# A first transform stage that contracts 128 rows from 128-byte runs, with B's first half in two pieces and zero matmuls ahead of the data

## The chip, the cores and the metric

The kernel runs on one core of one Trainium2 chip. A core has TensorE (PE, matmuls into PSUM), VectorE (DVE), ScalarE (ACT), GpSimd (POOL), SyncE (SP, which here only issues transfers) and 16 DMA engines that all queues share. The metric is the time of one execution on the device in microseconds, the median over runs.

## The reference, cut to what matters

Two independent halves are computed on a sequence of 2048 steps with 640 channels and put side by side in the output, in bf16.

```python
# A: a diagonal state space with complex states
Lam_bar = exp(dt * Lam);  B_bar = ((Lam_bar - 1) / Lam)[:, None] * Bmat
h_t = Lam_bar * h_{t-1} + x_t @ B_bar.T
a = 2 * real(h @ Cmat.T) + x * Dskip
# B: a short shift convolution, a product, and a convolution as long as the sequence
kv = (sum_t k_pad[t : t + S] * shift_k[:, ks - 1 - t]) * v
y = irfft(rfft(kv, 2 S) * rfft(ssm_k, 2 S))[:S]
b = q * (y + kv * ssm_D)
out = concat([a, b], -1)
```

## The kernel before, in words

**Half A** works on 16 interleaved phases of the sequence. B is loaded with a transposing DMA (`a_B`, operations `B00` to `B11`: first digit the half of the 640 states, second digit real or imaginary part), x likewise (the first eight phases come plainly as `xn0`, `xn1` and are turned on TensorE by `px..`, emptied by `ex..`; the others as `x1..`, transposing DMAs). `a_unit` (line 646) projects: for ten groups j of states and two halves, `dn0_j_h` and `dn1_j_h` are ten matmuls each (line 658), `e1` empties PSUM, `m1` and `e3` combine phases by rotation matrices (`set_..`, line 416). A coarse scan (`S`, `jw`, `scan`, `jv`), a way down (`d1`, `d00` to `d02`, added by DVE in `a1`, `a0`) and the output projection `py` (line 801, emptied by `ey`, stored by `st`) follow. C is loaded by transposing DMAs `cn..` and scaled by `ct..`.

**Half B** goes in five groups G of 128 channels. The convolution over 2 x 2048 points is a transform in two stages, with tables made on the chip. For each group the filter (`h`) and the product (`k`) go through the same steps:
- `hst` (line 828) loads the filter from HBM, `dtap` (line 831) adds ssm_D to the first tap. `kvs`, `kvl` (lines 888, 890) write the product kv, which DVE and ACT made in `cv`, `cs`, `ca`, `cm`, to HBM and load it again, so that 64 partitions hold 8 channels times 8 stretches of time, twice.
- `s1` (line 894) is the first stage: four operations of 32 matmuls, each on 64 rows by 64 columns of the array (form 64*64), two accumulating on each result. `e1h`, `e1k` empty them on ACT or DVE through the helper `copy` (lines 237, 239).
- `s2` (line 919) is the second stage, 16 matmuls each of 128 rows by 64 columns (128*64), emptied by `e2`.
- `pP`, `pQ`, `pY` multiply the spectra, `i2` (64*128) and a transposing DMA `zt` and `i1` (128*64) go back, `ob` multiplies by q and stores.

**Order.** All operations go through a graph, but the order is a text, `ORDER` (line 146): a list of names. `x/A`, `x/D`, `x/G`, `x/S` name the engine where there is a choice, and the digits behind `@` are the buffers that the operation takes (PSUM pairs of banks, or one of seven SBUF buffers `s4` and six `s8`). `emit` issues each engine's share in the order of that list, so each engine, and each queue of transfers, works strictly in order. `halves` and `split` (lines 108, 120) let operations that can be run either way (`m1`, `d0`, `d1`, `S`, `jw`, `jv`; helper `mm`, line 227) take two matmuls of 128*64 instead of one of 128*128 where the operation before them on TensorE is of that form.

The tables of the first stage are made in `setup`: phases `w0`, `w1` (lines 449, 454), sines `w2` (470), masks `mk` (481), the table `R` (490), and `Ct` for the way back (498).

Of the kernel before, what the change touches and what calls it, by code (L numbers as in the profile page):

```python
# [9 lines left out]
ALU = mybir.AluOpType  # L10
ACT = mybir.ActivationFunctionType
# [30 lines left out]
class Graph:  # L42
# [77 lines left out]
    def halves(self, o):  # L120

        return True if o.name.startswith(("dn", "s2", "i1")) else False if o.name.startswith(("py", "px")) else None
# [24 lines left out]
ld_lre kz2/D@0 w0 xn0@0 scol pidx Dm0 B00 consts J0 w1 E0 kz1/G@1 ci0@1 w2 zero J1 c4 wi1@2 ld_lim ld_ldt xn1@2 wi0@3 bc  # L147
px00@0 B01 px02@1 wm1 nrow ex00/A ex02/A par@2 px04@3 p0 nrowf dtb Dm1/S wm0 B10 px10@0 ex04/A px12@1 E1 px14@2 p1 ex12/A nrho
x121 fi mk rn ph ci1 ld_sk/S dn0_2_0@4 x130 ex10/D trig dn0_0_0@6 B11 ex14/D ws1@4 R dn1_2_0 rc ss dn1_1_0@0 set_3_0/D
set_2_0/G dn1_0_0 e1_2_0/A dn1_4_0@2 set_1_0/D ws0@5 k0@6 kz0/G set_1_1/G x131 dn0_4_0 e1_0_0/D hst0/S@2 m1_2_0 x120 set_3_1/G  # L150
dn0_1_0 e3_2_0/D e1_4_0/D m1_0_0 dn1_8_0@4 ct@3 set_2_1/G e3_0_0/D e1_1_0/D dn0_8_0 sk x101 cv300/D@4 dn1_9_0@6 set_4_1/D
m1_1_0 dn0_9_0 cs200/D@3 v0@5 e1_8_0/A dtap0/D set_8_1/D m1_4_0 e3_1_0/A m1_8_0 e3_4_0/A ca200 s1h03@0,4 x100 e3_8_0/A s1h01@2
e1h03/A dn0_3_0@4 cs100/D x111 e1h01/A ca100 s1h00@0 x110 e1_9_0/A s1h02@2 cs000/D dn1_3_0 kz3/G@2 e1h00/A ca000 hst1/S@6
m1_9_0 e1h02/A dn1_7_0@0 cm00 e1_3_0/A s2h02@2,5 den kvs0/S dn0_7_0 e3_9_0/A k1 e2h02/A set_12_0/D s2h03@6 m1_3_0 g e2h03/A
dn0_4_1@2 e1_7_0/A s2h01@6 dn1_4_1 e2h01/A dtap1/D set_G_0/G set_8_0/D m1_7_0 e3_3_0/A kvl0/S@3 s1h10@6,0 e3_7_0/A k2 s1h12@4
e1h10/A set_G_1/D dn0_0_1@0 set_12_1/G e1h12/A s1h11@6 set_4_0/D dn1_0_1 e1_4_1/A ld_dsk/G e1h11/A m1_4_1 cv310/D@5 s1h13@4
e3_4_1/A cs210/D@4 v1@6 s1k03@6,2 e1h13/A dn0_1_1@2 ca210 e1k03/A s1k00@4 cs110/D e1_0_1/A s1k02@6 V dn1_1_1 e1k00/D e1k02/A
m1_0_1 ca110 e1_1_1/A s2h00@4 s1k01@6 e3_0_1/A cs010/D m1_1_1 e1k01/A dn1_3_1@0 cv320/D@3 e3_1_1/A ca010 s2k03@6,1 e2h00/A
dn0_3_1 cm10 e2k03/A s2k01@2,4 s2k00@4 e2k01/A kvs1/S dn1_2_1@6 e2k00/D k3 e1_3_1/A s2k02@2 pP00@6 s2h11@4,1 e2k02/A dn0_2_1
pQ00 e2h11/A m1_3_1 cn00@3 dn0_8_1@2 e3_3_1/A pP01@5 e1_2_1/A s2h12@4 s2h13@0 pY00 e2h12/A dn1_8_1 e2h13/A m1_2_1 pQ01  # L160
kvl1/S@4 i200@4,4 e3_2_1/A i201@0 e300/A pY01 S0@6 v2@6 e301/A dn1_9_1@4 cs220/D@1 eS0/A ca220 i202@0 e1_8_1/A i203@6 cn10
dn0_9_1 cs120/D e302/A ca120 e303/A s1k10@0,2 m1_8_1 cs020/D e1_9_1/A zt0@5 dn1_6_1@6 e3_8_1/D e1k10/A ca020 m1_9_1 s1k11@2
e3_9_1/A s1k13@0 cm20 e1k11/A s1k12@4 dn0_6_1 e1k13/A e1k12/D jw0@2 e1_6_1/A s2h10@0 q0/S@5 jsw0 dn0_7_1@4 cn11@0 e2h10/A Ct
jcw0 jaw00 scan0 hst2/S@0 s2k13@2,1 s2k12@0 e2k13/A dn1_7_1 e2k12/A dn1_5_0@2 e1_7_1/A s2k11@0,4 pP11@6 cn01 dn0_5_0 e2k11/A
pQ11 m1_7_1 s2k10@0 e3_7_1/A m1_6_1 e2k10/A pY11 dn1_6_0@4 e1_5_0/A i100@0 pP10@1 kvs2/S e3_6_1/A dn0_6_0 dtap2/G ob00 m1_5_0
s1h22@6,4 e3_5_0/A pQ10 e1_6_0/A s1h20@0 dn1_5_1@2 e1h22/A pY10 dn0_5_1 e1h20/A kz4/G@3 k4 diagD hst3/S@4 jv0@6 e1_5_1/A
i213@0,2 jsv0 m1_6_0 e313/A m1_5_1 i211@6 e3_5_1/D e3_6_0/A i212@0 jcv0 e311/A i210@2 kvl2/S@6 jav00 S5@4 v3@1 jav01 e312/A
e310/D d1_0@6 eS5/A ct00@0 a1_0 ct01@2 ect00/A jw5@4 jcw5 s1h23@6 ect01/A dtap3/D jsw5 ct10@0 e1h23/A ct11@2 jaw50 i101@4
scan5 ect11/A ct20@6 ect10/A s1h21@2 ect20/A s1k23@0,1 q1/S@0 ob01 e1h21/A d1_2@6 d1_3@7 a1_2 jv5@4 ob0/S e1k23/A ct21@2 zt1@5
jsv5 ect21/A ct30@0 jcv5 s1k21@4 jav51 ect30/A s1k22@2 jav50 d1_4@6 e1k21/A a1_3 d1_9@0 d1_5@1 a1_4 e1k22/A d1_7@7 a1_9 d1_6@6  # L170
ct31@4 a1_5 ct40@2 ect31/A d1_1@0 a1_6 d1_8@1 a1_7 ect40/A ct41@4 d00_6@6 a1_8 ect41/A d00_7@7 d00_0@2 a1_1 d00_5@3 cs230/A@5
d00_2@1 d00_8@0 a00_5 py0_32@4,0 a00_6 a00_2 py1_32 a00_7 a00_8 s1k20@6 ey_32/A a00_0 d00_9@3 d00_4@1 e1k20/A st_32/S d00_3@0
a00_9 d00_1@2 i111@4 a00_1 cv330/A@6 a00_3 i110@6 a00_4 s1h33@2,0 ca230 py0_03@0,1 e1h33/A ob11 cs130/A py1_03 ob10 py0_33@2,0
ey_03/A ca130 st_03/S ob1/S py1_33 cs030/D ca030 d01_1@4 s1h32@6 ey_33/A a01_1 s1h30@0 st_33/S e1h32/A cm30 d01_9@5 hst4/S@2
d01_3@4 py0_02@2,1 cv340/A@5 cs240/D@1 kvs3/S a01_9 py1_02 e1h30/A ca240 d01_0@5 py0_00@6,0 ey_02/D cs140/A a01_0 st_02/S
dtap4/G s2h20@0,3 a01_3 d01_8@5 s2k21@2,0 e2h20/A a01_8 d01_6@4 py1_00 kvl3/S@6 ca140 e2k21/A a01_6 s2k20@0 ey_00/A d01_5@5
d01_2@4 e2k20/A d02_6@2 st_00/G a01_5 s2h21@6 d01_4@3 a02_6 d01_7@5 e2h21/A py0_31@0,1 a01_7 cs040/A a01_2 s1k33@6,2 a01_4
s1k30@4 s1k32@2 pP20@3 e1k30/A py1_31 e1k32/A ca040 py0_12@4,0 e1k33/A pQ20 q4/S@1 ey_31/A py1_12 pY20 st_31/S d02_5@2 s2h23@6
v4@0 ey_12/A a02_5 d02_3@3 s2h22@0 e2h23/A a02_3 d02_1@2 d02_7@4 d02_2@5 a02_1 e2h22/A s1k31@6 st_12/S a02_2 d02_9@3 e1k31/A
s1h31@0 a02_9 d02_4@2 a02_7 d02_8@5 e1h31/A s2k22@6,6 d02_0@3 a02_8 e2k22/A i220@0,5 a02_4 i221@4 a02_0 e320/A s2h33@6,4 cm40  # L180
s2h30@2 py0_21@0,1 e2h30/A e2h33/D kvs4/S e321/A py1_21 s2k23@2 ey_21/A s2h32@6 e2k23/D st_21/S s1h40@4,1 e2h32/A s1h42@0
kvl4/S@4 pP21@3 s2k31@2,0 e1h42/A py0_20@6,0 e2k31/D e1h40/A s2k32@0,5 pQ21 s2k33@4 e2k32/A s2h31@2 py1_20 pY21 e2k33/A pP31@6
py0_22@0,1 ey_20/A e2h31/A st_20/S pQ31 s1h41@4 s1k40@6,0 pY31 s1h43@2 e1k40/A py1_22 q2/S@2 e1h41/D e1h43/A s2k30@6 ey_22/D
s2h41@2,3 e2k30/A i223@4 st_22/G e2h41/D s1k41@0 e323/A s1k42@6 pP30@5 py0_13@2,0 e1k42/A pQ30 e1k41/A py1_13 pY30 s1k43@4
i222@6 ey_13/D e1k43/A i231@0,2 e322/D st_13/S i232@2 e331/A s2k40@4,4 e332/D s2k41@6 zt2@4 e2k40/A s2h42@0 e2h42/D e2k41/A
s2h40@2 i230@4 e2h40/A i233@6 e330/D py0_30@0,1 e333/A pP40@0 s2h43@2 s2k42@4,3 pQ40 zt3@1 e2h43/A s2k43@6 py1_30 pY40 e2k42/A
e2k43/A py0_23@2,0 ey_30/A pP41@5 i121@4 pQ41 st_30/S q3/S@6 i240@6,0 i241@0 pY41 e340/A py1_23 e341/A i242@6 ey_23/A i243@0
e342/A st_23/G i120@2 e343/D py0_10@6,1 ob20 zt4@5 ob21 i131@0 i130@2 ob31 py1_10 ob30 ob2/S py0_11@4,0 ey_10/D st_10/S ob3/S
py1_11 i140@0 ey_11/A st_11/G i141@2 ob40 py0_01@6,1 ob41 py1_01 ob4/S ey_01/A st_01/S
# [3 lines left out]
class Kernel:  # L193
# [55 lines left out]
    def pre(self):  # L249
        op, v = self.op, self.nc.vector  # L250
        self.Dm = self.t([128, 80], bf16, "Dm")

        def f_Dm(e):
            v.memset(self.Dm[:], 0.0)
        op("Dm0", {"DVE": 0.1}, f_Dm, w=["Dm"])
        op("Dm1", {"SP": 0.4, "POOL": 1.2}, lambda e: self.eng[e].dma_start(
            out=self.Dm[0:128:16, :], in_=self.B_ssm_D.rearrange("(b c) -> c b", c=8)), w=["Dm"], dma=0.5)

    def setup(self):
# [69 lines left out]
        small("nrow", f_nrow, [], ["nrow"], 0.3, "POOL")  # L329
        small("nrowf", lambda: v.tensor_copy(out=nrowf[:], in_=nrow[:]), ["nrow"], ["nrowf"], 0.5)  # L330
# [112 lines left out]
        ws = T([128, 96], i32, "ws")  # L443
        rowa = T([128, 2], f32, "rowa")
        colw = T([128, 1], f32, "colw")
        pr = T([128, 2], i32, "pr")
        phs = T([128, 96], i32, "phs")

        def f_w0():
            g.iota(ws[:, 0:64], pattern=[[0, 2], [4, 32]], base=1, channel_multiplier=0)  # L450
            g.iota(ws[:, 64:96], pattern=[[1, 32]], base=0, channel_multiplier=0)
        small("w0", f_w0, [], ["ws"], 0.4, "POOL")

        def f_w1():
            v.tensor_single_scalar(out=pr[:, 0:1], in_=pidx[:], scalar=15, op=ALU.bitwise_and)
            v.tensor_single_scalar(out=pr[:, 1:2], in_=pidx[:], scalar=31, op=ALU.bitwise_and)
            v.tensor_scalar(out=rowa[:, 0:1], in0=pr[:, 0:1], scalar1=2.0, scalar2=0.0, op0=ALU.mult, op1=ALU.add)
            v.tensor_scalar(out=rowa[:, 1:2], in0=pr[:, 0:1], scalar1=2.0, scalar2=1.0, op0=ALU.mult, op1=ALU.add)
            v.tensor_scalar(out=colw[:], in0=pr[:, 1:2], scalar1=4.0, scalar2=1.0, op0=ALU.mult, op1=ALU.add)
            for a0 in range(2):  # L460
# [714 lines left out]
```

## Time and profile before

| what | value |
|---|---|
| median of 6 runs | 202.2 us (201.65 to 205.76) |
| the profiled execution | 201.83 us, its span 200.0 us |
| busy: PE, DVE, ACT, POOL | 186.9, 168.2, 148.1, 21.1 us |
| matmuls | 4042 recorded |
| s1 matmuls (L909) | 1280, 22.8 us |
| s2 matmuls (L945) | 640, 42.8 us in two groups |
| dn matmuls (L658) | 400, 49.8 us |
| packets on the queue of SP and ACT | 109668, 32.52 MB |

The span runs from the first to the last instruction; the 1.83 us outside it belong to the execution but to no instruction. A busy time of TensorE counts overlapping matmuls once, and their ends are modelled, so starts of one group and of the next are what tells its length. "Chain" is the list of work that ended last, followed back from the end: start, length, engine, tile and line. In the timeline, the last bracket of a line is the idle time of the engine before it and what ended it.

### The profile page before, as it was taken

The numbers are of one execution on the slowest core, as the hardware profiler recorded it, in microseconds if no ns is written. First come the engines' busy times: TensorE is split into PE (matmuls) and PEld (weight loads), VectorE is DVE, ScalarE is ACT, GpSimd is POOL, SyncE is SP. The second block draws the span as 40 slices with busy tenths as digits, with TensorE's granted clock in tenths as the row PEclk, the third lists the DMA queues.
The fourth block names the chain that finished last, engine by engine and source line by source line (L and its number), as shares of the span: only waits on it lengthen the run. The fifth ranks groups of instructions, "written<-read, shape, count | busy, mean of one in ns | idle before, by whom it ended". The sixth has DMA issues, their size and how long they took to land.

```text
span 200.0 us, 8858 instructions
## 1 busy us (share of the span) xinstructions
PE 186.9 (93%) x4042; PEld 138.2 (69%) x4043; DVE 168.2 (84%) x264; ACT 148.1 (74%) x175; POOL 21.1 (11%) x35
## 2 busy tenths in 40 slices
PE   0889999998999999799999999999999999999992
PEld 0756676656777677567657777677787878788771
DVE  7899899876889999959988999788959999977640
ACT  4999978996888888489976749896967678753011
POOL 8056500800000000000000000100000010001010
PEclk9999999999999999999999999999999999999999
DMA  6999996999989999969994058508334243998995
GB/s 172 264 156 191 190 167 155 240 147 139 215 209 208 167 237 200 261 136 215 226 207 107 5 147 252 136 26 184 94 143 108 76 101 90 185 221 186 202 239 143
DMA packets 109959, 33.74 MB, mean 169 GB/s; under 512 B 107106, under 2 KB 108642, under 8 KB 109922
## 3 DMA queue, kind: packets, MB, share of 16 engines
q1 hardware_dynamic: 109668, 32.52, 81.3%
q8 instruction: 31, 0.51, 1.0%
q0 software_dynamic: 224, 0.66, 1.0%
q14 instruction: 6, 0.05, 0.1%
q10 hardware_dynamic: 30, 0.00, 0.0%
HBM read 9.19 MB, written 7.86 MB: 85 GB/s over the span
## 4 chain that ended last, share of the span: by engine, by line
PE 69%; DMA 12%; ACT 7%; DVE 7%; issue 2%; SPq 1%; POOL 0%; POOLq 0%; DVEq 0%; ACTq 0%
PE ps L806 18%; PE ps L658 16%; PE ps L909 9%; PE ps L945 8%; DMA s<-kvd 5%; PE ps L1001 5%; PE ps L231 4%; DMA s<-s 4%; PE ps L233 4%; PE ps L1037 3%; DMA s<-in_B_ssm_k_dram 3%; ACT s L237 2%; PE ps L810 2%; DVE s L239 2%; DVE s L968 1%
## 5 line engine op out<-in xcount | busy, mean ns | idle before, releaser
L237 ACT CAST s<-ps 128x1024 bf16<-128x1024 f32 x86 | 84.0, 1018 | 16.6 <-PE ps L909 6.4
L658 PE MATMUL ps<-xT,BC 128*64 128x512 bf16 x400 | 49.8, 386 | 0.5 <-DVE xT L239 0.5
L806 PE MATMUL ps<-BC,hb 128*128 128x320 bf16 x240 | 36.4, 300 | 0.0
L658 PEld LDWEIGHTS <-BC 128*64 128x64 bf16 x400 | 24.0, 111 | 14.5 <-issue 1.9
L806 PEld LDWEIGHTS <-hb 128*128 128x128 bf16 x240 | 21.9, 98 | 8.7 <-issue 0.3
L968 DVE TENSOR_TENSOR s<-s,s 128x2048 bf16<-128x2048 bf16 x20 | 24.5, 1223 | 2.4 <-ACT s L237 0.7
L237 ACT CAST yo<-ps 128x640 bf16<-128x640 f32 x12 | 8.4, 697 | 22.3 <-PE ps L810 18.1
L909 PE MATMUL ps<-R,s 64*64 64x128 bf16 x1280 | 22.8, 218 | 1.5 <-POOL s L831 1.2
L239 DVE CAST s<-ps 128x1024 bf16<-128x1024 f32 x14 | 17.0, 1222 | 7.8 <-ACT hb L237 2.2
L909 PEld LDWEIGHTS <-s 64*64 64x64 bf16 x1280 | 18.7, 107 | 7.0 <-issue 4.4
L945 PE MATMUL ps<-s,Wim 128*64 128x128 bf16 x320 | 21.3, 219 | 0.7 <-issue 0.7
L763 DVE TENSOR_TENSOR hb<-ps,hb 128x512 bf16<-128x512 f32 x30 | 19.1, 685 | 2.9 <-PE ps L231 1.6
L945 PE MATMUL ps<-s,Wre 128*64 128x128 bf16 x320 | 21.5, 221 | 0.0
L945 PEld LDWEIGHTS <-Wre 128*64 128x64 bf16 x320 | 18.2, 110 | 2.5 <-issue 0.4
L945 PEld LDWEIGHTS <-Wim 128*64 128x64 bf16 x320 | 18.2, 110 | 1.9 <-issue 0.8
L884 DVE TENSOR_TENSOR s<-s,s 128x2048 bf16<-128x2048 bf16 x15 | 18.3, 1222 | 1.0 <-ACT s L876 0.7
L1044 DVE TENSOR_TENSOR s<-ps,s 128x1024 bf16<-128x1024 f32 x10 | 11.8, 1218 | 3.6 <-PE ps L1037 3.5
L237 ACT CAST hb<-ps 128x768 bf16<-128x768 f32 x17 | 13.7, 808 | 1.1 <-PE ps L658 1.1
L968 DVE TENSOR_TENSOR s<-s 128x1024 bf16<-128x1024 bf16 x20 | 13.8, 690 | 0.3
L231 PE MATMUL ps<-hb,M 128*64 128x256 bf16 (+1 forms) x136 | 13.4, 296 | 0.0
L876 ACT ACTIVATE s<-s,sk 128x2048 bf16<-128x2048 bf16 x6 | 12.0, 2006 | 0.4 <-DVE s L884 0.4
L806 PE MATMUL ps<-BC,Qb 128*128 128x320 bf16 x80 | 12.2, 300 | 0.0
(157 smaller groups left out, 261.1 us busy)
## 6 DMA issues: line engine op xcount, KB each, us to landing
s<-in_B_ssm_k_dram SPq DMA_DIRECT2D x5, 512.0 KB, 5.4
kvd<-s SPq DMA_DIRECT2D x5, 512.0 KB, 3.6
s<-kvd SPq DMA_DIRECT2D x5, 512.0 KB, 5.2
s<-in_B_q_dram SPq DMA_DIRECT2D x5, 512.0 KB, 4.5
out_dram<-s SPq DMA_DIRECT2D x5, 512.0 KB, 5.2
out_dram<-yo SPq DMA_DIRECT2D x12, 160.0 KB, 2.8
s<-in_A_x_dram SPq DMA_DIRECT2D x2, 640.0 KB, 4.4
out_dram<-yo POOLq DMA_DIRECT2D x4, 160.0 KB, 3.4
```

What stands on the lines that cost most here:

```text
L231: self.nc.tensor.matmul(out[h], lhsT=lhsT[:, h], rhs=rhs, **k)
L237: self.nc.scalar.copy(out=out, in_=in_)
L239: self.eng[e].tensor_copy(out=out, in_=in_)
L658: nc.tensor.matmul(P[64 * ri:64 * ri + 64, b, :], lhsT=self.BT[:, k, ri, 64 * j:64 * j + 64], rhs=self.xT[:, k, hf, 2 * b:2 * b + 2, :].re ...
L763: v.tensor_tensor(out=hv(r), in0=self.P(p2)[:, 0, :].rearrange("p (h m) -> p h m", h=2), in1=hv(r), op=ALU.add)
L806: nc.tensor.matmul(P[:, part, 0:320], lhsT=hap(j), rhs=self.CT[:, j, c0:c0 + 320], start=(j == 0), stop=False)
L876: nc.scalar.activation(out=out, in_=k(j), func=ACT.Copy, scale=self.sk[:, G, j:j + 1])
L884: op(f"ca{j}{G}{h}", {"DVE": dve_tt(W_)}, lambda e, c=c, tt=tt: v.tensor_tensor(out=c(), in0=c(), in1=tt(), op=ALU.add), r=[f"tm{G}{h}"], ...
L909: nc.tensor.matmul(P[64 * ri:64 * ri + 64, r, 128 * b4:128 * b4 + 128], lhsT=d[64 * r:64 * r + 64, 4 * qd + b4, a0, :], rhs=self.R[64 * r: ...
L945: nc.tensor.matmul(P[64 * pi:64 * pi + 64, ri, 128 * k4:128 * k4 + 128], lhsT=W[:, kp, pi, :], rhs=A[:, kp + 16 * pi, :], start=True, stop ...
L968: v.tensor_tensor(out=o, in0=a, in1=b, op=op_)
L1044: v.tensor_tensor(out=o, in0=self.P(pt)[:].rearrange("p s (b a c) -> p a (s b) c", b=8, a=16), in1=o, op=ALU.mult)
```

## The change

- `s1` contracts all 128 partitions. `hst` and `kvl` lay out 4 channels times 32 stretches of 64 steps on the partitions, so that one DMA run is 64 values (128 bytes) instead of 128 (256 bytes). An operation is 16 matmuls of form 128*64 that don't accumulate, and `halves` counts it among those of that form. `R`, the masks and phases shrink with it; `Dm` grows from 80 to 160 columns, and `dtap` touches 32 places instead of 16.
- B comes in three pieces of 128, 192 and 320 states, two transfers each, instead of two halves of 320.
- `wz` clears a corner of xT that later holds x's second half, and `warm` runs eight matmuls of 128 x 512 on it, first on TensorE.
- `ORDER` is written anew as a whole: other places, other engines and other buffers for most operations.

```diff
-        return True if o.name.startswith(("dn", "s2", "i1")) else False if o.name.startswith(("py", "px")) else None
+        return True if o.name.startswith(("dn", "s1", "s2", "i1")) else False if o.name.startswith(("py", "px")) else None
...
+        def f_warm(e):
+            for _ in range(8):
+                nc.tensor.matmul(self.P(warm)[:, 0, :], lhsT=self.xT[:, 0, 1, 0, 0:128], rhs=self.xT[:, 0, 1, 0:2, :].rearrange("p r m -> p (r m)"),
+                                 start=True, stop=True)
+        op("wz", {"POOL": 0.45, "DVE": 0.3}, lambda e: self.eng[e].memset(self.xT[:, 0, 1, 0:2, :], 0.0), w=["x10", "x11", "wz"])
+        op("warm", {"PE": 1.9}, f_warm, r=["wz", "x10", "x11"], w=["warm"], bufs=[warm], due=-35)
...
-        for h in range(2):
+        for h, (lo, n) in enumerate(((0, 128), (128, 192), (320, 320))):
...
-            in_=self.B_ssm_k[c0:c0 + 128, :].rearrange("(b c) (a t) -> (c a) b t", c=8, t=128)), w=[f"sth{G}"], bufs=[st], dma=2.4)
+            out=self.S4(st)[:, 0:2048].rearrange("p (b t) -> p b t", b=32),
+            in_=self.B_ssm_k[c0:c0 + 128, :].rearrange("(b c) (a t) -> (c a) b t", c=4, t=64)), w=[f"sth{G}"], bufs=[st], dma=3.8)
...
-            in_=d.rearrange("(b c) (a t) -> (c a) b t", c=8, t=128)), r=[f"kvd{G}"], w=[f"stk{G}"], bufs=[st], dma=2.4)
+            in_=d.rearrange("(b c) (a t) -> (c a) b t", c=4, t=64)), r=[f"kvd{G}"], w=[f"stk{G}"], bufs=[st], dma=3.8)
...
-                for b4 in range(4):
-                    for a0 in range(2):
-                        for r in range(2):
-                            for ri in range(2):
-                                nc.tensor.matmul(P[64 * ri:64 * ri + 64, r, 128 * b4:128 * b4 + 128],
-                                                 lhsT=d[64 * r:64 * r + 64, 4 * qd + b4, a0, :],
-                                                 rhs=self.R[64 * r:64 * r + 64, a0, ri, :], start=(a0 == 0), stop=(a0 == 1))
+                for b in range(8):
+                    for ri in range(2):
+                        nc.tensor.matmul(P[64 * ri:64 * ri + 64, b // 4, 128 * (b % 4):128 * (b % 4) + 128], lhsT=d[:, 8 * qd + b, :],
+                                         rhs=self.R[:, ri, :], start=True, stop=True)
```

Parts of the new order that the prediction speaks of (of the lines of the list, the names in the places told):

```diff
+ld_lre consts w0 xn0@0 pidx wz/D ld_lim J0 w1 ld_ldt E0 warm@0 wi1@0 xn1@1 B00 w2 kz2/G@1 J1 kz3/G@2 wi0@3 nrow c4 ci0@2
+px00@1 B01 par@0 px04@2 ex00/A px02@3 zero B10 kz0/G@4 kz1/D@5 bc nrowf p0 wm0 dtb x120 px14@0 px10@4 E1 ex02/A px12@5 p1 fi
+B11 ex04/A nrho ph Dm0 ci1 rn B20 scol dn0_1_0@6 ex14/D ex12/D dn0_0_0@2 ex10/D trig Dm1/S wm1 B21 dn1_1_0 ws0@6 dn1_0_0 rc ss
...
+m1_7_0 dtap0/G e1_8_0/A m1_3_0 g m1_9_0 x111 e3_7_0/A m1_8_0 e3_3_0/A s1h01@2,4 e3_9_0/A s1h00@4 x131 e1h01/A s1h03@0
+set_G_1/D e1h03/A s1h02@2 v0@0 cv300/D@6 e1h00/A cs200/D@3 dn1_4_0@0 ca200 e1h02/A dn0_4_0 k1 cs100/D e3_8_0/A s2h02@4,5
...
+e1h13/A s1h11@0 ca010 dn1_4_1 v1@5 e1h11/A cv320/D@4 e1_2_1/A s2h13@2,1 s2h11@0 e1_4_1/A e2h13/D m1_2_1 e2h11/A m1_4_1 V
+s2h10@2 e3_4_1/D e3_2_1/D s1k00@0,2 e2h10/A s1k02@6 e1k00/D s1k03@4 e1k02/A s1k01@2 e1k03/D s2h12@0 e1k01/A dn0_1_1@6 cm10
...
+kz4/G@0 jav01 k4 i211@0 e313/A jcw5 jw5@6 i101@4 jsw5 e311/A ct00@2 jaw50 i210@6 ob01 ect00/A d1_3@0 e310/A ct01@2 scan5
+ct10@4 ect01/A ct11@6 d1_0@1 ect11/A ct20@2 a1_0 ect10/A ct21@6 zt1@1 ect20/D ect21/A ct30@4 d1_1@1 jcv5 ect30/A s1k23@2,2
```

## The prediction

> **What bounds the kernel now.** I read the page's slices first, then the chain that ended last, then the timeline of the first 22 us, then the DMA issues.
>
> ```profile
> span 200.0 us, 8858 instructions
> ...
> PE   0889999998999999799999999999999999999992
> ...
> DMA  6999996999989999969994058508334243998995
> ...
> q1 hardware_dynamic: 109668, 32.52, 81.3%
> ```
>
> TensorE is nearly full from the third slice to the last but one; the DMA engines are just as full for the first 105 us and half idle after that. I then lined up the matmul records with the order list. From the first projection unit (dn0_2_0, 10.71 us) to the end of the last output matmul (196.37) are 185.7 us. With each kind of operation at its undisturbed row (dn 1.08, s1 and s2 0.44, i1 1.01, py 1.50, m1 0.33 us) and 0.115 us for each change of form (below), the work in that stretch is 178.4 us. So 7.3 us are waits and a slow start. **The kernel ends when TensorE's list is done; only what shortens that list, starts it earlier or removes one of its waits counts.**
>
> ```profile
> 25.40 1.08 PE ps L658 x10
> ...
> 27.13 1.02 PE ps L909 x64
> 28.15 1.20 PE ps L658 x10
> ...
> 52.62 0.89 PE ps L945 x32
> ...
> 76.68 1.07 SPq L775
> 77.85 5.12 DMA s<-in_B_ssm_k_dram
> 83.14 0.33 POOL s L831
> ```
>
> In this piece of the chain a dn unit (ten matmuls, L658) takes 1.08 us among its like and 1.20 between two s1 groups (L909). Two s1 operations take 1.02 us; two s2 operations (L945), as much streaming in dn's form, take 0.89. One change of form thus costs about 0.12 us, most of it on leaving. The last three lines are a transfer that TensorE waits for: hst2, late because SP was held in the issue of a C transpose (L775).
>
> ```profile
> 8.47 2.31 PE L607 MATMUL ps<-ident,s 128*128 128x128 bf16 x20 [0.74 <-DMA s<-in_A_x_dram]
> ...
> 9.61 0.57 ACT L237 COPY xT<-ps 128x512 bf16<-128x512 bf16 x1
> ...
> 10.71 3.25 PE L658 MATMUL ps<-xT,BC 128*64 128x512 bf16 x20
> ...
> 11.56 2.31 DVE L487 TENSOR_SCALAR mk<-mk 128x4 f32<-128x4 f32 x1
> ...
> 13.78 1.01 DVE L239 COPY xT<-ps 128x1024 bf16<-128x1024 bf16 x2
> ...
> 14.51 5.59 PE L658 MATMUL ps<-xT,BC 128*64 128x512 bf16 x50 [0.55 <-DVE xT L239]
> ```
>
> At the start, twenty matmuls take 3.25 us where later ones take 2.16 and a drain of 0.2: 0.9 us too many. In the records a pair is 427 ns apart until 12.4 us and 216 ns after it. Then TensorE has nothing until 14.51 (0.7 us), because the copy of xT stood on DVE behind a mask operation that took 2.31 us beside a GpSimd multiply.
>
> **The change, part by part.**
>
> *Stage s1 in 128 rows.* An s1 operation goes from 32 matmuls of 64*64 to 16 of 128*64. The streaming is the same (eight slots of 128 columns). The s2 row is the new form exactly: 0.443 to 0.447 us against 0.446 to 0.471 for s1 now, so the operation itself I cost at nothing. What goes is the changes of form: walking both order lists gives 95 now and 64 then (s1 joins dn, s2, i1 and most m1). 31 x 0.12 = **-3.7 us**, all on the path. 584 matmuls and as many weight loads fewer to fetch I cost at nothing; the chain has 2% "issue".
>
> *128-byte runs.* Ten loads (hst, kvl) of 512 KB go from 2048 packets to 4096. The page has no such load. From below: 0, the bytes are the same. From above: each new packet as dear as the mean packet of q1 (0.813 x 16 x 200 us / 109668 = 23.7 ns), 2048 x 23.7 / 16 = +3.0 us each.
>
> ```profile
> s<-in_B_ssm_k_dram SPq DMA_DIRECT2D x5, 512.0 KB, 5.4
> kvd<-s SPq DMA_DIRECT2D x5, 512.0 KB, 3.6
> s<-kvd SPq DMA_DIRECT2D x5, 512.0 KB, 5.2
> ```
>
> Nearest row: the same 512 KB takes 3.6 us in 128 runs of 4 KB and 5.2 in 2048 of 256 B; 1920 packets cost 1.6 us, so 2048 more cost **+1.7 us** a load. I take that, and 0 and 3.0 for the range. [...]
>
> *Start.* SP issues x's two halves and the small loads first, then B in pieces of 128, 192 and 320 states. Ahead of the first dn stand two x halves (2.0 us of DMA each by their packets) and two pieces of 164 KB (0.8 each) after a first landing delay of 2.8: about 8.4 us, where B01 landed at 10.72 before. So B no longer decides; ACT does. Its list is unchanged up to there: w2's sines end at 6.28, then ex00 0.95, the exp table and dtb 1.41, ex02 0.95, ex04 0.57: 10.2 us. The first dn starts 0.5 us earlier. On DVE the mask work leaves the place ahead of xT's copies; by the rows they end near 11.9, before TensorE needs them at 12.3: the 0.7 us go. The eight zero matmuls start when DVE has cleared xT's corner (about 1.4) and at 427 ns each end at 4.9, when x lands (4.88); they cost nothing, and if they end later the slack up to ACT's 10.2 covers them. With the clock up, 0.9 us go: **-2.1 us**. If zeros don't raise the clock, 0.9 come back. The change adds one wait on SP: x120 overwrites the cleared corner and so waits for the eight matmuls. It stands behind B10 in SP's queue, which SP reaches after 5 us, and behind it wait B11 and B20; a matmul that ended late would hold those, wanted at 14 and 20 us.
> [...]
>
> *The new order in the stage from 10 to 50 us.* PE's list now brings more units early, and the engines that empty PSUM must keep up. ACT after ex04, by start-to-start rows: rn 1.7, trig 0.55, ws0 3.25, two e1 1.4, ct 3.8, e1 0.7, ws1 3.25, three e1 2.1, three e3 1.05, then e1h at 0.93 each: dn1_4_0, which needs e1h03's buffer, waits 0.4 us. **+0.4.** DVE, by its rows, is through e3_2_0 at 20.0 us as the list has it; from there to the end of cm00 stand five set and G halves 5.2, small tables, den, g and an evacuation 4.5, and the shift convolution 7.9 (four scalings of 0.75, four adds or products of 1.22): 37.6, against 32.8 now. On to e2h13 are seven operations of the next convolution 6.65, two sets 2.0, the taps 0.35 and two evacuations 1.65: 48.2. TensorE wants that buffer for s2h10 at 46.7 (36.0 us of its list after a virtual start of 10.7): 1.5 us of waiting. kvl0 follows: 10.4 us from the issue of kvs0 to landing now, plus 1.7, from 37.6: 49.7, wanted at 48.6: 1.1 us. Before had 0.38 and 0.86 us of waits there (s1h13 to s1k03; s2h00). Net **+1.4**.
>
> *hst2* is moved ahead of three of the four C transposes, and s1h20 needs it near 74 us: issued near 64, landed by 72 at 5.4 + 1.7 us. The 1.25 us that m1_5_0's successor waits go: **-1.25**. Its price falls on cn00, cn10 and cn11, needed at ct00 near 88.
>
> *Nothing:* smaller R, mk and w1 (DVE, before 14 us), the wider Dm, 32 instead of 16 taps (0.35 us on an engine with gaps), split evacuation shapes (same 1024 elements: 1.02 us on ACT).
>
> Sum: -3.7 - 2.1 + 0.4 + 1.4 - 1.25 = -5.25 us, with the other waits of some 3 us kept. The tail (last matmul, cast 0.7, store to 200.0) is the same in kind. The profiled execution took 201.83 us for its span of 200.0; it would be 196.6. The median of the runs shown is 202.2, 0.4 above it: **197.0**.
>
> **Rivals.**
> *A, the start is kept whole:* ACT and DVE keep up and 128-byte runs cost little: -3.7 - 2.1 - 1.25 - 1.24 = -8.3, **193.9**. For it: the order was drawn up anew around these lengths. Against: both engines are full in the slices from 10 to 30 us.
> *B, the buffers take it back:* new waits of some 4 us in place of the switches, about **201.5**. For it: DVE 84% and ACT 74% busy, DMA full to 105 us; six of the ten slower loads fall in that time.
> *C, slower: zt1 lands late.* Its packets end at 107 us now and i111 starts at 108.96 without a wait; then TensorE wants i111 near 103. Ahead of it six loads grow by x each, and four transfers (v3, hst3, q1, ob0) are moved behind it, 3.0 us each by the mean packet: 6x - 12.1 against now. After i111 both lists are alike (84.3 and 83.7 us), so from 6x - 12.1 = 2.6, x = 2.45 us, the kernel is slower. At the upper bound, 3.0, it is 3.5 us slower: **205.7**.
> *D, it doesn't do what it says:* zeros leave the clock down: 197.9. It lies in the forecast's range.
>
> **Chances.** Forecast (195.5 to 200) 0.50 with D in it; A 0.14; B 0.24 (half of it under 201.2); C 0.12. About 0.5%, 1.0 us, is what a measurement of this kernel can tell from no change. Faster 0.76, same 0.12, slower 0.12. The range reaches from near A to past B's middle: 194.0 to 202.0.
>
> **What would show it.** Right: dn units at 1.08 us beside s1; some 64 changes of form; a first dn near 10.2 us with pairs at 216 ns; no wait for s<-in_B_ssm_k_dram near 80; kvl and hst at about 7 us to landing. Wrong: s1 operations over 0.47 us among their like; loads 2.5 us longer; TensorE waiting near 103 us for s<-s; a first dn at 427 ns a pair; or waits on DVE and ACT between 25 and 60 us of more than 4 us.

## The result

| | median | profiled execution | its span |
|---|---|---|---|
| before | 202.64 us | 201.83 us | 200.0 us |
| after | 203.94 us | 204.15 us | 202.4 us |

The ratio after to before is 1.0036, with a 95% interval of 1.0013 to 1.0058: no gain, and by this ratio a loss of 0.1 to 0.6%, where 197.0 us and a range of 194 to 202 were forecast. The ratios compare only the faster executions of each kernel, so they are not the quotients of the medians. The two profiled executions lie 2.3 us apart, the medians 1.3. The page of the kernel after, slices, queue and shares of the chain:

```profile
span 202.4 us, 7698 instructions
...
PE   6699787999999899997999989999999999999792
...
DMA  5997997999999999999999976980599195677956
...
q1 hardware_dynamic: 129088, 32.33, 94.2%
...
PE 61%; DMA 17%; ACT 9%; DVE 8%; issue 2%; SPq 0%; POOL 0%; DVEq 0%; ACTq 0%
```

TensorE has two slices of 7 between 20 and 35 us, where before has 9; as many bytes take 94.2% of the DMA engines instead of 81.3%; and transfers are 17% of the chain (before 12%). Yet the two gains that were forecast on TensorE are there, as the chain (start, length, what) and the timeline of TensorE show:

```profile
71.11 1.08 PE ps L657 x10
72.19 0.89 PE ps L906 x32
```
```profile
8.27 1.29 PE L607 MATMUL ps<-ident,s 128*128 128x128 bf16 x20 [1.66 <-DMA s<-in_A_x_dram]
9.49 9.04 PE L657 MATMUL ps<-xT,BC 128*64 128x512 bf16 x80
```

A dn unit takes 1.08 us beside s1 operations, and two of these 0.89 (before: 1.20 and 1.02). The first dn starts at 9.49 with the clock up (its first pairs go 240 and then 216 ns apart); allowing for the slow start of before, TensorE's list begins 2.9 us earlier. Walking the list as in the prediction, with each kind at its undisturbed row (below: its like), gives 174.8 us for 178.4. So 6.5 us were gained. The other way go the waits behind the start: 14.2 us for 5.5. TensorE's waits by who ended them (sum, times, longest):

```profile
PE ps L657 <- DMA BC<-in_A_B_im_dram: 1.9, 1, 1.9
PE ps L906 <- POOL s L830: 1.6, 1, 1.6
PE ps L785 <- DMA s<-in_A_C_re_dram: 1.4, 1, 1.4
...
PE ps L809 <- issue: 1.2, 1, 1.2
...
PE ps L906 <- DMA s<-kvd: 0.8, 1, 0.8
```

Matched with the order list: dn0_7_0 stops 2.0 us for the last transpose of B (B21, landed 21.61); s1h01 1.8 us for hst0 and its taps; s1k10 0.9 for kvl1; ct01 1.5 for the C transpose that SP issues last (at 88.8); s1h03 and s1h02 0.85 together for ACT; d01_1's successor 0.9 for VectorE, which had waited for q1; and in the last 13 us 1.6 us of "issue", idle time with no engine and no transfer at its end (none there before; it has 0.7 elsewhere). The wait for hst2 (1.2) is gone, and so are those at s2h00 (0.9) and for kvl0 behind s1h13 (0.4).

### The profile page after: what moved, and what is told of

The parts are those of the page before. It is cut to its first block, busy times and chain, and to the rows that moved or that the text cites. A ratio compares the mean times of both kernels' runs of the same rounds, so it can differ in the third digit from the quotient of the medians.

```text
span 202.4 us, 7698 instructions
## 1 busy us (share of the span) xinstructions
PE 185.7 (92%) x3458; PEld 137.3 (68%) x3459; DVE 167.8 (83%) x261; ACT 147.5 (73%) x173; POOL 18.0 (9%) x32
## 3 DMA queue, kind: packets, MB, share of 16 engines
q1 hardware_dynamic: 129088, 32.33, 94.2%
## 4 chain that ended last, share of the span: by engine, by line
PE 61%; DMA 17%; ACT 9%; DVE 8%; issue 2%; SPq 0%; POOL 0%; DVEq 0%; ACTq 0%
PE ps L805 19%; PE ps L657 12%; PE ps L940 8%; PE ps L906 7%; DMA BC<-in_A_B_im_dram 4%; ACT s L238 4%; PE ps L1032 4%; DMA s<-in_B_q_dram 4%; PE ps L996 3%; DMA s<-kvd 3%; DMA s<-in_A_C_re_dram 3%; PE ps L232 3%; DMA s<-in_B_k_dram 3%; PE ps L809 2%; PE ps L234 2%
## 5 line engine op out<-in xcount | busy, mean ns | idle before, releaser
L238 ACT CAST s<-ps 128x1024 bf16<-128x1024 f32 x88 | 85.1, 1017 | 17.3 <-PE ps L906 6.2
L657 PE MATMUL ps<-xT,BC 128*64 128x512 bf16 x400 | 47.6, 380 | 2.3 <-DMA BC<-in_A_B_im_dram 1.9
L657 PEld LDWEIGHTS <-BC 128*64 128x64 bf16 x400 | 24.3, 110 | 17.3 <-DMA BC<-in_A_B_im_dram 2.5
L906 PE MATMUL ps<-R,s 128*64 128x128 bf16 x640 | 22.3, 220 | 2.8 <-POOL s L830 1.6
L906 PEld LDWEIGHTS <-s 128*64 128x64 bf16 x640 | 19.6, 110 | 5.6 <-POOL s L830 1.9
L238 ACT CAST yo<-ps 128x640 bf16<-128x640 f32 x11 | 7.6, 688 | 20.8 <-PE ps L809 16.9
L240 DVE CAST s<-ps 128x1024 bf16<-128x1024 f32 x12 | 14.6, 1222 | 3.6 <-PE ps L996 1.6
L238 ACT CAST hb<-ps 128x768 bf16<-128x768 f32 x18 | 14.2, 799 | 3.6 <-PE ps L657 3.4
L232 PEld LDWEIGHTS <-M 128*64 128x64 bf16 x252 | 12.3, 110 | 2.5 <-issue 1.1
L877 DVE TENSOR_SCALAR s<-s,sk 128x2048 bf16<-128x2048 bf16 x14 | 10.5, 752 | 4.0 <-DMA s<-in_B_k_dram 3.5
```

The lines of the kernel that those rows point to most:

```text
L232: self.nc.tensor.matmul(out[h], lhsT=lhsT[:, h], rhs=rhs, **k)
L238: self.nc.scalar.copy(out=out, in_=in_)
L240: self.eng[e].tensor_copy(out=out, in_=in_)
L657: nc.tensor.matmul(P[64 * ri:64 * ri + 64, b, :], lhsT=self.BT[:, k, ri, 64 * j:64 * j + 64], rhs=self.xT[:, k, hf, 2 * b:2 * b + 2, :].re ...
L906: nc.tensor.matmul(P[64 * ri:64 * ri + 64, b // 4, 128 * (b % 4):128 * (b % 4) + 128], lhsT=d[:, 8 * qd + b, :], rhs=self.R[:, ri, :], sta ...
```

## The experiments

Ratios are to the kernel before on the same chip, with their intervals; the chips differ between runs, so runs of different chips compare by ratio. Waits are those of one profiled execution, which can lie 2 us to either side of its run's median (e2 210.33, e10 203.07, e13 203.76). e1, e3 and e16 price the 256-byte runs only: their first stage sums other rows than it should. Theories 1 to 3 are those named in e1's expectation, theory 4 that of e12's.

| run | median us | ratio |
|---|---|---|
| after | 203.94 | 1.0036 (1.0013 to 1.0058) |
| e1 new order, new stage, 256-byte runs | 200.39 | 0.9863 (0.9799 to 0.9928) |
| e2 old order, new stage, 128-byte runs | 212.41 | 1.0497 (1.0430 to 1.0564) |
| e3 old order, new stage, 256-byte runs | 200.15 | 0.9866 (0.9805 to 0.9926) |
| e4 new order, old stage | 208.27 | 1.0253 (1.0185 to 1.0320) |
| e5 Dm later | 206.33 | 1.0202 (1.0133 to 1.0271) |
| e5b the same again | 206.46 | 1.0200 (1.0125 to 1.0275) |
| e6 no zeros | 202.69 | 1.0007 (0.9958 to 1.0057) |
| e7 B in two halves | 202.13 | 0.9962 (0.9915 to 1.0008) |
| e8 before, with zeros | 202.27 | 1.0008 (0.9964 to 1.0051) |
| e9 Dm in four rows | 201.73 | 0.9956 (0.9913 to 0.9999) |
| e10 e9, q1 ahead of ob0 | 201.66 | 0.9953 (0.9906 to 1.0001) |
| e11 e9 without zeros | 203.34 | 0.9980 (0.9941 to 1.0020) |
| e12, e13, e14: e10 with 24, 48, 72 small matmuls | 203.36, 201.64, 200.04 | 1.0076, 0.9974, 0.9940 (each within 0.0044) |
| e15 e10, kvl1 ahead of k3 | 204.72 | 1.0123 (1.0075 to 1.0171) |
| e16 e14 with 256-byte runs | 199.11 | 0.9805 (0.9754 to 0.9856) |
| e17 before, with 24 small matmuls | 201.89 | 0.9955 (0.9915 to 0.9995) |

### The runs, the stage and the order (e1 to e4)

```diff
# e1, e3: hst and kvl on the layout of before
-  rearrange("p (b t) -> p b t", b=32) <- "(b c) (a t) -> (c a) b t", c=4, t=64
+  rearrange("p (b t) -> p b t", b=16) <- "(b c) (a t) -> (c a) b t", c=8, t=128
# e2, e3: ORDER, halves of B and start of before, no zeros; e4: s1, tables, Dm of before
```

> The changed kernel with the ten loads of the first stage (hst, kvl) back on 256-byte runs, as before; all matmuls, casts and the order of work are as in the changed kernel, and so the first stage sums other rows than it should (part of the computation is changed). Theory 1 (the 20480 additional packets load the DMA engines, and what shares them lands late): DMA time falls by some 28 us of 16 engines' span share (from 94% to about 81%), about 5 of the roughly 8 us of waits for transfers go, and the time falls from 203.9 to about 199. Theory 2 (the opening transfers, and the two-byte load of Dm ahead of B21, are what makes B21 and hst0 late): 3.7 us at dn0_7_0 and s1h01 stay, the time is 202 to 203. Theory 3 (the new places in SP's queue cost, not the runs): within 0.5% of the changed kernel.

> The kernel before with the new first stage alone: 128 rows from 128-byte runs, the operation order, the halves of B and the start as before, no matmuls on zeros. Nominal sum of TensorE's list 3.6 us shorter (61 changes of form for 92). Theory 1 (the runs cost): new waits for hst, kvl and what shares the DMA engines take most of it back, 201 to 203 against 202.6. Theory 2 and theory 3 (the start, or the new order): the old order keeps its waits of 5.5 us, and the 3.6 us come out, about 199.

> The run before this one with 256-byte loads, so that the first stage sums other rows than it should (part of the computation is changed): the shorter list of TensorE without the price of the runs, in the old order. Theory 1: about 199, 3.6 us under the kernel before and 2 to 4 us under the same order with 128-byte runs. Theories 2 and 3: 199 as well, and the same as with 128-byte runs.

> The changed kernel with the old first stage: 64 rows a matmul from 256-byte runs, its tables and the 80-column Dm, in the new order, with B in three pieces and the matmuls on zeros. TensorE's list is 4.4 us longer than the changed kernel's (99 changes of form for 61) and its start 2.9 us earlier than before's. Theory 1: of the additional waits of 9 us about 5 go, 203 to 204. Theory 2: B21 (2.0 us) is late only if the transfers of the opening are to blame, which here are alike but for Dm (5 elements a run of bytes for 10): 2 us of wait there stay, 205 to 206. Theory 3 (the new order): nearly all the waits stay and the longer list comes on top, about 208.

The page of e1: span, the queue's share and the loads (KB each, us to landing); then the loads of after.

```profile
span 198.8 us, 7697 instructions
...
q1 hardware_dynamic: 108608, 32.33, 86.3%
...
s<-in_B_ssm_k_dram SPq DMA_DIRECT2D x5, 512.0 KB, 4.1
...
s<-kvd SPq DMA_DIRECT2D x5, 512.0 KB, 4.9
```
```profile
s<-in_B_ssm_k_dram SPq DMA_DIRECT2D x5, 512.0 KB, 5.6
...
s<-kvd SPq DMA_DIRECT2D x5, 512.0 KB, 5.3
```

The ten loads cost 0.942 x 202.4 - 0.863 x 198.8 = 19.1 us of all 16 engines, 1.9 a load; in after they land 1.5 and 0.4 us later than in e1. In the new order that is worth 1.7% (203.94 to 200.39, 3.5 us), and in e1's profile the waits for hst0, kvl1 and q1 are gone, while B21's stays (1.9 us at dn0_7_0). In the old order the same runs cost 12.3 us (212.41 against 200.15). There SP gets to kvl0 late (issued at 40.7 us for 36.8, landed at 47.9 for 42.6) and TensorE has nothing else to do; waits for kvd, and the granted clock, of e2, then the waits of e3:

```profile
PEclk9999999995999999999999999999999999999999
```
```profile
PE ps L897 <- DMA s<-kvd: 4.6, 2, 4.3
```
```profile
PE ps L897 <- DMA s<-kvd: 1.4, 1, 1.4
```

After the wait that ends at 47.9 the next units run at the lower clock until 52.6 (the slice with the 5 is that from 46.9 to 52.1 us): s1k03, dn0_1_1, s1k00 and s1k02 take 2.3 us over their like.

So **theory 1 holds for the runs** (e1, e2, e3), and the price of one and the same load depends on the order: 0.35 us each in the one, 1.2 in the other. Theory 3 is refuted by e1 as far as it put the whole loss on the order: in the new order, too, the time falls once the runs are as before. But e1 and e3 have the same ratio (0.9863, 0.9866): with 256-byte runs the new order, with its earlier start and without the wait for hst2, gains nothing over the old one. e4 hit theory 3's number, 208, for another reason. Its waits:

```profile
PE ps L916 <- issue: 3.8, 3, 2.2
PE ps L952 <- issue: 2.2, 1, 2.2
```

Transfers are 2% of its chain; 7 us in all are idle time without a releaser, more than half of it in the stage whose matmuls are twice as many, and behind one of these stops the granted clock is 0.5 from 153.8 to 157.2 us. That was in no theory, and led to the fourth.

### Dm and the start (e5 to e9, e11)

```diff
# e5, e5b
- ... B20 scol dn0_1_0@6 ... trig Dm1/S wm1 B21 ...   ld_sk/S hst0/S@3
+ ... B20 scol dn0_1_0@6 ... trig wm1 B21 ...          ld_sk/S Dm1/S hst0/S@3
# e6, e11: wz/D and warm@0 left out.  e8: wz/D and warm@0 put into before
# e7: for h, (lo, n) in enumerate(((0, 320), (320, 320))); B20, B21 left out
# e9: Dm is [128, 640], its partition 32c holds D[c:c+637]
- out=self.Dm[0:128:32, :], in_=self.B_ssm_D.rearrange("(b c) -> c b", c=4)
+ out=self.Dm[0:128:32, 0:637], in_=bass.AP(..., ap=[[1, 4], [1, 637]])
- in1=self.Dm[:, 32 * G:32 * G + 32]
+ in1=self.Dm[:, 128 * G:128 * G + 128:4]
```

> The changed kernel with one operation moved: the load of Dm (640 elements of two bytes into 4 partitions) stands ahead of hst0 in SP's queue and no longer ahead of the last transpose of B. Theory 2 (that load holds up B21): B21 is issued 0.7 us earlier and lands by 19.5 instead of 21.6 us, the 2.0 us wait at dn0_7_0 goes, and the time falls by about 2 us, to 202, or by up to 3 if hst0 comes earlier as well. Theory 1 (the 128-byte runs are the whole of it): none of the ten loads runs before 24 us, so B21 lands where it did, and the time is that of the changed kernel within 0.5%.

> The kernel with Dm ahead of hst0 once more, since its profiled execution was over three times as long as the others and shows nothing of the order. Theory: B21 lands by 19.5, but the two-byte runs now stand ahead of hst0 and of the next transposes, hst0 and its taps are ready 2 to 4 us later than in the changed kernel, and the first stage waits for them near 30 us: 205 to 206. Rival: the time of the last run was an effect of that chip or that moment, and it is 201.5 to 202.5.

> The changed kernel without the matmuls on zeros and the clearing ahead of them. By the prediction they are worth 0.9 us: the first dn operations at the lower clock. By the traces of before and after, the start as a whole gained 2.86 us: if the zeros carry it all, the first dn operations start near 10.3 and run at 427 ns a pair, and the time rises by 2 to 3 us where nothing behind it waits. Rival: B21 and hst0 hold TensorE at 21.6 and 29.5 us whatever it did before, so that what is lost at the start comes out of those waits, and the time is the same within 0.5%.

> The changed kernel with B in two halves as before (four transposes for six), in the places of the first four. The prediction gave the pieces nothing, since ACT decided when the first dn starts. If so, the first dn starts at about 10 us all the same; the second half is issued at 9.6 to 11 us instead of 13.5, lands by 18, and the wait of 2.0 us at dn0_7_0 goes: about 202. Rival: the larger first transposes land 1 to 1.5 us later and with them the first dn, so that the gain at dn0_7_0 is in part paid at the start: 203 to 204.

> The kernel before with the matmuls on zeros alone, in its own order. By the prediction's step the clock is up when the first dn runs: 0.9 us of the 1.6 us that dn0_2_0 and dn0_0_0 take over their like go, 201.7 against 202.6. Rival: what ACT and the buffers give later sets the pace, and the 0.9 us come back as waits before 45 us: the same as before within 0.3 us.

> The changed kernel with Dm loaded as four shifted rows of 637 elements in one run each, in the same place of SP's queue, instead of 640 runs of two bytes; the taps are then read with a stride of four. Nothing else differs. Theory 2 (the two-byte runs through 4 partitions stall SP's queue and the transposes behind them): the last transpose of B is issued in about 1.3 us instead of 4.2 and lands by 18.5 instead of 21.6, hst0 is issued by 22 instead of 24.1, the waits at dn0_7_0 (2.0) and s1h01 (1.7) go, and the time falls by 2.5 to 3.7 us, to about 201. Rival (the transposes themselves, six for B, are what SP and the DMA engines are slow with): B21 lands within 1 us of where it did, and the time falls by less than 1 us.

> The run with Dm in four rows, without the matmuls on zeros. If the zeros are worth the 0.9 us of the prediction once nothing behind them holds TensorE, this is 0.9 us slower than the run with Dm alone (up to 1.7, by the first dn at 10.35 and its 0.75 us at the lower clock in the run without zeros). Rival: waits between 25 and 50 us take the 0.9 us back also here, and the two are the same within 0.3 us, or this one is faster, as the changed kernel was without the zeros (202.7 against about 203.6).

One execution of e5, the profiled one, took 647.81 us, its matmuls 3 to 4 times as far apart as in after; the others took 204.7 to 207.1. e5b is the same kernel again. SP's issues around Dm in after, in e4 (Dm of before, 8 partitions) and in e9:

```profile
12.79 0.68 SPq L257 DMA_DIRECT2D Dm<-in_B_ssm_D_dram  x1
13.52 4.23 SPq L633 DMA_TRANSPOSE BC<-in_A_B_im_dram  x1
```
```profile
13.35 3.06 SPq L641 DMA_TRANSPOSE BC<-in_A_B_im_dram  x1
```
```profile
12.78 1.55 SPq L633 DMA_TRANSPOSE BC<-in_A_B_im_dram  x1
```

The transpose behind Dm holds SP for 4.2, 3.1 and 1.6 us; B21 lands at 21.61, 19.01 and 17.81. In after the DMA engines start 323 packets between 18 and 20 us, right behind the 640 two-byte ones (16.3 to 17.3), single packets of 256 bytes taking up to 1.75 us; in e9 1048 in the same two microseconds. (Stretches with few packets occur without two-byte runs too: 685 between 28 and 30 us in e9.) With Dm in rows both waits, dn0_7_0's and s1h01's, are gone, and the ratio falls from 1.0036 to 0.9956, some 1.6 us. Moved ahead of hst0 (e5b), Dm stalls hst0 instead:

```profile
23.20 8.41 DMA s<-in_B_ssm_k_dram
```
```profile
PE ps L906 <- POOL s L830: 4.6, 1, 4.6
```

e5's expectation of a gain was wrong, e5b's of 205 to 206 close; but SP was held 3.7 us at B21 there without Dm ahead, so the hold is not Dm's alone. What Dm delays is the landing: the x transpose behind B21 lands at 19.9 us in e5b and at 23.0 in after. (A first stretch of long packets, between 14 and 18 us, is in all these runs.) Behind the wait for hst0 the granted clock of e5b is 0.5 from 32.5 to 35.9 us, 1.7 us more. **Theory 2 holds for the two-byte runs, wherever they stand**; what they do inside the DMA engines the trace doesn't show.

*The zeros.* In e8 the first dn starts at 9.49 instead of 10.71, and at 14.50 both are at the same place: dn0_0_0's successor waits 1.6 us more for the copy of xT (2.2 for 0.55). The rival was right, nothing is gained. In e6 the first dn starts at 10.35 and loses 0.75 us against units of 1.08, and the kernel is no slower: B21, landed at 20.16, no longer makes TensorE wait. With Dm repaired (e11 against e9) the zeros carry 1.6 us by the medians and 0.5 by the ratios, but the intervals overlap and e11 has 1.2 us more of "issue", so their price stays unsettled. Halves of B (e7) bring the first dn 1.9 us later, and stop it behind its first matmul:

```profile
11.37 0.64 PE L657 MATMUL ps<-xT,BC 128*64 128x512 bf16 x1
12.89 2.35 PE L657 MATMUL ps<-xT,BC 128*64 128x512 bf16 x20 [0.88 <-DMA BC<-in_A_B_im_dram]
```

x's second half lands 0.9 us later there (9.09 for 8.22), the transposes take 2.31 us for 1.29, and then B01 is awaited. Yet e7, having no wait at dn0_7_0, is not slower than after but 0.7% faster, with intervals that just miss each other. Its time is the 202 us of its expectation, the early start named there did not come. So in this order B's pieces did not pay.

### SP's queue (e10, e15)

```diff
# e10, on e9
- hst3/S@5 ... ob0/S a1_9 ... q1/S@3
+ hst3/S@5 ... a1_9 ... q1/S@3 ob0/S
# e15, on e10
- kvs1/S ... k3 ... kvl1/S@3
+ kvs1/S ... kvl1/S@3 k3
```

> The run before this one with one transfer moved as well: the load of q1 stands ahead of the store of ob0 in SP's queue, where it waited behind a store that waits for VectorE (issued 103.96, over after 4.1 us). Theory (a load that stands behind a waiting store is late): q1 lands some 3 to 4 us earlier, the 1.0 us that TensorE waits near 119 us goes, and the time is 1.0 us under the run with Dm alone. Rival: the DMA engines are full there, the store is then late, and the difference is under 0.5 us.

> The run with Dm in four rows and q1 ahead of ob0, with one more transfer moved: kvl1 stands ahead of the transposed load of k3 in SP's queue, and no longer behind it. Theory (the order in SP's queue decides which stage waits): kvl1 is issued some 1.3 us earlier, the 1.3 us that s1k10 waits near 68 us go, and the time is 0.5 to 1.3 us under the run with the two other edits, about 200.8. Rival: SP now stands still until kvs1 has landed, k3 and what is behind it come 2 to 3 us later, and the wait reappears at the next load: no difference.

The aimed-at wait went each time and another came. In e10 d01_1's 1.3 us (e9) are gone and s1k10 waits 1.3 for 0.4; the time is the same. In e15 s1k10's 1.3 fell to 0.4, and s1h20 then waits 1.6 us for hst2. Its ratio is 1.7% over e10's, more than the 0.6 us between their two profiles (e10's profiled execution is 1.4 us over its median), so the full cause is open. The rival holds in both: with the DMA engines as full as here (q1 94.2% of them in after), one load came early at another's cost.

### Where the instructions fall (e12 to e14, e17)

```diff
+ op("fill", ...): 24, 48 or 72 x matmul(P(fill)[0:64, 0, 0:10], lhsT=ident[:, 0:64], rhs=ident[:, 0:10])
- px02@3 zero
+ px02@3 fill@7 zero          # e17, in before: px04@3 fill@7
```

> The run with Dm in four rows and q1 ahead of ob0, and 24 matmuls of 64 by 10 put where TensorE waits for the second half of x (near 7 us, some 1.8 us of idle time): they do nothing but move all later instructions of TensorE by 48 places. Theory 4 (TensorE runs out of instructions where a block of 16384 bytes ends in a stage of short matmuls): the idle time of 2.9 us at py1_11 and py0_01 moves to another place or changes by over 0.5 us, other stretches stay. Rival (the transfers of that time, stores and transposes, hold the instruction blocks up): it stays in its places and within 0.5 us.

> The same with 48 such matmuls, 96 places. Theory 4: the idle time in the last 15 us differs from those with none and with 24, between 0.3 and 3.5 us, and the times of the runs follow it. Rival: within 0.5 us of the run without them.

> The same with 72 such matmuls, 144 places. Theory 4: one of the three shifts leaves under 1 us of idle time in the last 15 us. Rival: within 0.5 us of the run without them. Each of the three may lose up to 0.5 us at the start, if the fill takes longer than the wait in which it stands.

> The kernel before with 24 matmuls of 64 by 10 behind its last transpose of the first part of x, which move its later instructions by 48 places. Theory 4: the kernel before has 0.4 us of idle time without a releaser in its last 15 us by the luck of its places; shifted, it has 1 to 3 us there or in another stage, and the time rises by as much, to 203 to 205. Rival: its longer list of TensorE gives the instruction blocks time enough wherever they end: the same idle time, and the same as before within 0.5 us.

The chain of after near its end:

```profile
189.90 1.22 issue
191.12 0.19 PE ps L809
```

A block of 16384 bytes on the queue that the page calls "q8 instruction" starts at 188.9 and is over at 189.8; TensorE stops in the middle of three equal matmuls and goes on 1.3 us behind it. This is so in every trace but e5's, 19 in all: they have 34 stops of TensorE without a releaser of 0.45 us and more, and each of them ends 1.2 to 1.6 us behind the end of such a block. Most of the blocks, 26 to 31 in a trace, stop nothing. Idle time of this kind in e12, e13 and e14:

```profile
PE ps L811 <- issue: 3.0, 2, 1.8
PE ps L1002 <- issue: 1.2, 1, 1.2
```
```profile
PE ps L1038 <- issue: 4.1, 3, 2.0
```
```profile
PE ps L1038 <- issue: 1.4, 2, 0.8
```

In e10 it stands at 188 and 193 us (2.6 in all). The small matmuls move it to 92, 113 and 187 (e12) and to 91, 111 and 185 (e13), and leave 1.4 us in e14, at 91 and 184. In e13 the stop at 185 costs twice, as the timeline shows:

```profile
186.19 0.69 PE L1038 MATMUL ps<-Ct,s 128*64 128x64 bf16 x23 [1.99 <-issue]
186.80 2.85 PE L811 MATMUL ps<-BC,hb 128*128 128x320 bf16 x10
```

Ten output matmuls take 2.85 us behind it, where they take 1.53 otherwise: the clock has gone down (granted 0.992 over this execution, 1.000 over after's). **Where the stops fall depends on the place in the code**, and of the three kernels the one with least is the fastest. That is not all of their difference: e12 and e13 have as much and lie 1% apart, and their early waits differ. And what the stops cost is not shown: e10 with 2.6 us of them and e14 with 1.4 have the same ratio within their intervals (0.9953, 0.9940). e17 got 2.4 us of "issue" for 0.7 and was not slower, since its waits before 100 us were some 2 us shorter, hst2's among them; why, isn't settled. (Its expectation put 0.4 us without a releaser at the end of before; that was a wait for a transfer, and before's 0.7 stands at 48 us.) That before owes its time to a lucky place is thus not shown.

### All three taken away (e16)

> The changed kernel with Dm in four rows, q1 ahead of ob0 and the 72 small matmuls, and the ten loads of the first stage back on 256-byte runs, so that this stage sums other rows than it should (part of the computation is changed). If the three prices are separate and are all that the forecast lacked, they add up: 200.0 to 200.4 less 3.5, about 197, which was the forecast. Rival: the waits that the runs cause are by now covered by others, and only 1 to 2 us come out, 198.5 to 199.5.

Of TensorE's waits in e16 this is the longest behind the start:

```profile
PE ps L1038 <- issue: 0.8, 2, 0.5
```

The median is 199.11, its profiled execution 197.90: nearer to the rival than to the sum. From e14 to e16 the ratio falls by 1.35%, 2.7 us, and not 3.5. After less e16 are 4.8 us of the 6.9 that the forecast lacked, for the runs, Dm, q1's place and the small matmuls together. The prices partly cover each other: the wait for hst0 goes in e1 and in e9 alike, so it stands in both. e16's first dn came at 11.44, 1.5 us later than in e14, behind twenty transposes that take 2.31 us for 1.29.

**The lowest ratio of a kernel that leaves nothing out is e14's**, 0.6% under before (0.2 to 1.0%): the change, Dm in rows, q1 earlier, and 72 small matmuls. Against e9 (0.9956) and e10 its advantage is within the intervals.

## Why the prediction was wrong, step by step

- *Form changes, -3.7:* right. The list is 3.6 us shorter, and e3 is 1.3% (2.7 us) under before with little else changed.
- *128-byte runs, +1.7 a load:* the size was right as engine time (1.9 us a load). As time to landing it was too large: 1.5 us for hst and 0.4 for kvl, which land after 5.6 and 5.3 us where about 7 were forecast. 128-byte packets take 13 ns in the median and 256-byte ones 18, so a byte costs 1.44 times as much. **What failed is the next step**, which let the 1.7 us delay only the load itself: in the sum it stands in kvl0's wait alone (part of the net +1.4, with e2h13's). Neither wait came; the 19 us of additional DMA time came out as waits for hst0, kvl1 and q1, 3.5 us by e1.
- *"Nothing: ... the wider Dm":* wrong, the second failed step. Not its 160 columns cost, but that 640 two-byte runs now go to 4 partitions and stand ahead of B21: about 1.6 us by e9, two waits of 2.0 and 1.8 in the profile. The prediction put at 20 us the time at which B20, the other transpose of that piece, is wanted, and priced a late landing of B21 nowhere.
- *Start, -2.1:* too little for what it is, -2.9 (first dn at 9.49, not 10.2). ACT does not decide, as the prediction had it: the first dn begins before ex04 is over (9.78), right behind the twenty transposes, which take 1.29 us for 2.31, and B01, expected by 8.4, lands at 9.49 only. That eight matmuls on zeros raise the clock no row had shown when 0.9 us was put on it, it was the author's estimate; e8 shows it: there the same transposes take 1.29 us for 2.31, and the first twenty matmuls of dn 2.84 for 3.25. But a gain at the start counts only if what comes next has landed; e6 and e8 show it given back within 20 us.
- *ACT, +0.4; DVE, +1.4 net:* s1h03 and s1h02 wait 0.85 together for ACT. DVE's wait did not come; and of the waits that were set against it, the 0.86 at s2h00 is idle time without a releaser in before.
- *hst2, -1.25:* right; s1h20 has no wait in after. But its price came too: ct01 waits 1.5 us for a C transpose that was moved behind hst2. The prediction named that price and gave it no term.
- *"The tail is the same in kind":* right; from the last matmul to the end are 3.7 us in both. *Fewer instructions "at nothing":* the sum had no term for stops without a releaser; after has 1.6 us of them in its last 13 us, before 0.7 in all. What that costs is not shown (e10, e14).
- *Rivals:* C's place was wrong (i111 starts at 109.7 without a wait). D did not happen here, but did elsewhere (below). B had the mechanism, new waits, at 4 us; it was 8.7 more, some 6 of them in the first 105 us.

The sum that came: -3.6 - 2.9 + 8.7 = +2.2 us, where the spans of the two profiled executions differ by 2.4 (the medians by 1.3).

## What to carry to other kernels

Where the DMA engines are as full as here (q1 86 to 94% of them in e2 and after), cost smaller runs by the engine time that they add to everything in the queue, not by the delay of their own landing: the same ten loads cost 3.5 us in one order and 12 in another. Look at each small transfer for its element runs and for who stands behind it; four long rows in place of 640 two-byte runs were worth 1.6 us. And when a number comes out as a theory said, read the waits before believing it (e4).

## What was unexpected of the hardware

- The clock raised by the zeros survives some waits and not others. Of 13 profiled executions with zeros, 10 have the twenty transposes ahead of the first dn in 1.29 us, with up to 1.66 us of waiting in front of them. Three took 2.2 to 2.3: e10 behind 1.77 us, e7 behind 2.38, and e16 right behind the 72 small matmuls.

```profile
8.19 2.23 PE L607 MATMUL ps<-ident,s 128*128 128x128 bf16 x20 [1.77 <-DMA s<-in_A_x_dram]
```

  Later stops differ too: the clock went down behind 1.99 (e13) and 2.34 us (e11), where the next ten output matmuls take 2.85 us, and stayed behind 1.81 (e12, nine in 1.38) and 2.07 (e6, ten in 1.53). In e4 it stayed behind a stop of 2.21 us and went down behind one of 2.16 (granted 0.5 from 153.8 to 157.2). So the length of a wait alone does not decide it here.
- A load of 640 two-byte runs was followed by two microseconds in which few packets start (323, and 1048 in e9, with four rows in its place).
- TensorE stands still up to 2.3 us (e11) with no releaser, and goes on 1.2 to 1.6 us behind the end of a 16384-byte block on the instruction queue, in all 34 stops of that kind. 48 more instructions at the start (e12) bring such stops to 92 and 113 us, where e10 has none before 188.
